# Handing PSUM banks from one stage to the next: which banks pass to whom, in a fused linear-attention and leaky-ReLU MLP kernel

## The chip, the cores and the metric

The kernel runs on one core of a Trainium2 chip. The metric is the device time of one launch in microseconds (us), the median of several runs. The engines are TensorE (PE, with its weight loads listed apart as PEld), VectorE (DVE), ScalarE (ACT), GpSimd (POOL) and SyncE (SP), which here only issues DMAs.

## The reference, cut to what matters

```python
def _attn_ref(q, k, v):                     # 8 batches, 8 heads, 576 tokens, 64 wide
    phi(x) = concatenate([relu(x) * cos_w, relu(x) * sin_w], axis=-1)
    kv = einsum('bhsf,bhsd->bhfd', phi(k), v)
    z = sum(phi(k), axis=2)
    num = einsum('bhsf,bhfd->bhsd', phi(q), kv)
    den = einsum('bhsf,bhf->bhs', phi(q), z)[..., None] + 1e-06
    return num / den

def _moe_ref(x, w_in, w_out):               # x: 4608 x 512, w_in: 512 x 2048, w_out: 2048 x 512
    h = x @ w_in
    g = maximum(0.01 * h, h)
    return g @ w_out
```

Inputs and output are float32; the kernel multiplies in float16 and accumulates in float32.

## The kernel before, in words

The 4608 rows are cut into nine groups of 512. Groups 0 to 7 are the first 512 tokens of each batch, and group 8 is made of the 64 last tokens of all eight batches (the "tail"). A group passes through these steps. `load_main`, `load_kvtail` and `load_qtail` bring q, k and v in as float32 (tiles `qst`, `kst`, `vst`, `ktl`, `vtl`, `qtl`). `k_part` and `q_part` make phi(k) and phi(q) in float16, `v_part` casts v; each of these can run on DVE or on ACT, and the strings of the table `ON` say which. `kv_all` multiplies phi(k) with v on PE and ACT copies the result. `q_transpose_dma` turns phi(q) by a transposing DMA, `num` multiplies it with kv on PE and divides on DVE (tiles `den`, `rden`, `xs`). `x_transpose_dma` turns the quotient; in group 2 alone PE turns it (`x_transpose`, line 490) and ACT copies it.

Then comes the MLP. Groups 0 and 1 are multiplied with w_in directly; from group 2 on w_in, and from group 1 on w_out, are multiplied by a seven-product (Strassen-Winograd) scheme on blocks of half the size. "Product one" in the words of the change is the multiplication with w_in, "product two" the one with w_out. In group 1 product one is `f1_pair` (line 833: pairs of 512-wide results in two PSUM banks, then a leaky ReLU by ACT at line 855). From group 2 on it is `p1(g, t, n, ...)`: set t of four, product n of seven, four matmuls 128 x 256 each, about which stand on ACT `seed` (line 892, copies a partial sum from one bank into another), `lrelu` (895), `u_copy` (902) and `u_lrelu` (909), and on DVE `u_add` (268). Product two is `p2(g, n, ...)` (line 975), with `o_copy` on ACT (994) and `o_add` on DVE (268). Sums of weight blocks (`w1_sums`, `w2_sums`), of x blocks (`x_sums`) and of g blocks (`g_sums`) run on DVE.

PSUM has eight banks of 512 float32 per partition, all in use. In the stage of groups 0 and 1 the pool `ps_h` has four (two tags of two banks, taken in turn by the pairs), `ps_o` has two single banks, and `ps_n` two. `x_transpose` of group 2 takes its bank from `ps_o`, `num` and `kv_all` theirs from `ps_n`. In the later stage four banks serve product one (`bank1`: two that the sets use in turn, then SEED and JOIN) and two serve product two (`bank2`). `open_banks` closes the first stage's pools and opens the later ones; a tile that lies on a bank of an old tile waits until that one's last reader is done. `open_seed` writes zeros into SEED by a matmul.

The order is a written table. Every call from group 1's product one on is put on a list with a place number out of `PLACE`, and the calls are issued in the order of these numbers. An engine works through its own instructions in that order, and SP its DMAs. The staging pool has three tiles for all loads of q, k and v from group 2 on: a load waits until a tile that has been read to the end is free, and what stands behind it on SP waits too.

Of the kernel before, what the change touches and what calls it, by code (L numbers as in the profile page):

```python
# [9 lines left out]
dt = mybir.dt  # L10
# [3 lines left out]
P = 128  # L14
# [4 lines left out]
def kernel(  # L19
# [26 lines left out]
    N2 = MAIN // 2  # L46
# [5 lines left out]
    first, first_ps = ExitStack(), ExitStack()  # L52

    def pool(name, bufs, space=None, stack=ctx):
# [5 lines left out]
    PS = bass.MemoryType.PSUM  # L60
# [15 lines left out]
    ps_of = {  # L76
        "h": pool("ps_h", 1, PS, first_ps),
        "o": pool("ps_o", 2, PS, first_ps),
        "n": pool("ps_n", 1, PS, first_ps),
    }  # L80
# [832 lines left out]
    SEED, JOIN = 2, 3  # L913
# [145 lines left out]
    bank1, bank2 = [], []  # L1059

    def open_banks():
        first_ps.close()
        ps_f1, ps_f2 = pool("ps_f1", 1, PS), pool("ps_f2", 1, PS)
        ps_of["n"] = pool("ps_m", 1, PS)
        for i in range(4):
            bank1.append(ps_f1.tile([P, 2, N2], dt.float32, name=f"ps_h{i}"))
        for i in range(2):
            bank2.append(ps_f2.tile([P, 2, N2], dt.float32, name=f"ps_o{i}"))

    def open_seed():  # L1070
        nc.tensor.matmul(
            bank1[SEED].rearrange("p h (a n) -> p (h a) n", n=P),
            lhsT=none,
            rhs=ident[:, None, :].broadcast_to([P, 4, P]),
        )
# [6 lines left out]
            16, 115, 251, 403, 570, 707, 852, 957,  # L1082
        ),
        "f1_pair": (
            52, 53, 46, 47, 43, 44, 39, 40, 25, 26, 57, 64, 17, 22, 35, 36,
        ),
        "open_banks": (
            72,
        ),
        "open_seed": (  # L1090
            73,
        ),
# [13 lines left out]
        ),  # L1106
        "seed": (
            81, 117, 149, 174, 237, 253, 304, 337, 399, 420, 452, 494, 535, 575, 609, 640, 690,
            710, 746, 790, 830, 865, 881, 911, 943, 967, 992, 1027,
        ),  # L1110
        "lrelu": (
# [4 lines left out]
        ),  # L1116
        "u_copy": (
# [4 lines left out]
        ),  # L1122
        "u_add": (
# [4 lines left out]
        ),  # L1128
        "u_lrelu": (
            154, 177, 247, 267, 288, 326, 377, 426, 444, 483, 556, 565, 602, 635, 696, 719, 768,  # L1130
            779, 828, 849, 888, 916, 931, 976, 998, 1025, 1048, 1065,
        ),
        "o_tiles": (
            97, 279, 406, 560, 720, 842, 974, 1066,
        ),
# [15 lines left out]
        ),  # L1151
        "o_copy": (
            98, 142, 171, 225, 280, 306, 348, 385, 407, 462, 475, 510, 561, 596, 617, 654, 721,
            756, 778, 820, 843, 886, 909, 951, 975, 1010, 1032, 1061, 1081, 1093, 1103, 1107, 1067,
            1086, 1096, 1114,
        ),
        "o_add": (
            160, 187, 230, 298, 349, 386, 417, 495, 521, 568, 634, 675, 730, 798, 825, 863, 919,
            953, 1003, 1036, 1056, 1087, 1111, 1119, 1090, 1098, 1116,
        ),  # L1160
        "o_store": (
            262, 342, 445, 423, 554, 646, 731, 682, 837, 900, 973, 989, 1080, 1057, 15, 111,
        ),
        "o_store_tail": (
            1092, 1112, 1115, 1120, 1117,
        ),
        "w1_sums": (
            102, 172, 67, 170, 175, 141,
        ),
        "w2_sums": (  # L1170
            10, 3, 42, 28, 38, 124, 164, 136,
        ),
        "g_sums": (
# [5 lines left out]
        ),  # L1179
        "kp_tiles": (  # L1180
            0, 69, 199, 358, 481, 622,
        ),
        "k_part": (
# [4 lines left out]
        ),  # L1188
        "v_part": (
            14, 13, 32, 129, 101, 103, 244, 255, 277, 323, 395, 389, 539, 553, 533, 672, 712, 663,  # L1190
        ),
        "kv_all": (
            41, 144, 281, 437, 566, 725,
        ),
        "q_part": (
# [4 lines left out]
        ),  # L1200
        "q_transpose_dma": (
            30, 21, 60, 9, 139, 92, 110, 89, 284, 260, 276, 295, 409, 413, 434, 422, 576, 538, 551,
            519, 698, 688, 748, 724, 805, 858, 872, 824,
        ),
# [138 lines left out]
```

## Time and profile before

| what | value |
|---|---|
| median of 3 runs | 271.7 us (271.56 to 272.0) |
| the profiled execution | 272.22 us, of which the span from its first to its last instruction is 270.4 us |
| granted TensorE clock | 1.000 |
| PE busy | 262.7 us |
| DVE busy | 207.7 us |
| ACT busy | 201.2 us |
| DMA, mean over the span | 211 GB/s, 57.05 MB |

Times below are counted from the span's start. Matmuls overlap in the trace, so PE looks busy while it waits a little. How long it stood is read from the starts: four matmuls of 128 x 256 start 0.437 us before the next thing (0.109 each), and four of 128 x 512 0.86 us before; what lies between two starts beyond that is waiting.

### The profile page before, as it was taken

The page shows a single profiled execution, that of the slowest core. Times are in us where ns is not written, and L with a number is a line of the kernel's source. Part 1 is how long each engine was busy: PE and PEld are TensorE (multiplying, and loading weights), DVE is VectorE, ACT ScalarE, POOL GpSimd, SP SyncE. Part 2 cuts the span into 40 slices and gives each one's busy share as a digit, 9 for nine tenths or more (in the row PEclk, how much of TensorE's full clock was granted, in tenths as well). Part 3 has the DMA queues.
Part 4 walks back from the last instruction along what each step waited for, and adds up shares of the span by engine and source line. Part 5 has one row for each costly group of instructions (what it writes and reads, how often), then busy time and mean ns, then how long its engine had stood idle before and what let it go on. Part 6 is the DMA issues. An engine that isn't in the chain of part 4 may idle for free.

```text
span 270.4 us, 6693 instructions
## 1 busy us (share of the span) xinstructions
PE 262.7 (97%) x2715; PEld 222.7 (82%) x2715; DVE 207.7 (77%) x429; ACT 201.2 (74%) x343; POOL 8.1 (3%) x20
## 2 busy tenths in 40 slices
PE   8899999998999999999999999999999999999994
PEld 3585565565889999999999999999988899999983
DVE  3984999996899988888877978888876845565651
ACT  7675545886899998987888977986777776774721
POOL 2131011000000000000000000000000000000000
PEclk9999999999999999999999999999999999999999
DMA  6999999989999999996999999789786060300134
GB/s 204 384 385 399 384 408 362 252 194 316 252 244 301 210 220 247 310 191 181 251 240 242 171 244 263 165 186 209 112 120 158 6 152 4 155 0 2 76 120 116
DMA packets 82654, 57.05 MB, mean 211 GB/s; under 512 B 54464, under 2 KB 75968, under 8 KB 82112
## 3 DMA queue, kind: packets, MB, share of 16 engines
q1 hardware_dynamic: 82320, 56.37, 83.2%
q8 instruction: 21, 0.34, 0.5%
q10 hardware_dynamic: 304, 0.26, 0.4%
q14 instruction: 9, 0.07, 0.1%
HBM read 36.70 MB, written 9.44 MB: 171 GB/s over the span
## 4 chain that ended last, share of the span: by engine, by line
PE 81%; DMA 10%; ACT 4%; SPq 1%; DVE 1%; issue 1%; POOL 0%; ACTq 0%; DVEq 0%
PE ps_o L975 30%; PE ps_h L882 29%; PE ps_o L543 5%; PE ps_h L506 4%; DMA vpr<-in_v_dram 3%; DMA vtl<-in_v_dram 3%; PE ps_h L975 3%; DMA qst<-in_q_dram 2%; PE ps_num L418 2%; PE ps_kv L317 2%; DMA qtl<-in_q_dram 2%; PE ps_hq L525 1%; PE ps_h L833 1%; ACT g L855 1%; PE ps_kvh L349 1%; PE ps_xth L475 1%
## 5 line engine op out<-in xcount | busy, mean ns | idle before, releaser
L975 PEld LDWEIGHTS <-g 128*128 128x128 f16 x640 | 62.3, 98 | 6.6
L268 DVE TENSOR_TENSOR u<-ps_h,u 128x512 f32<-128x512 f32 x56 | 38.5, 688 | 20.4 <-PE ps_h L882 15.3
L882 PEld LDWEIGHTS <-w 128*128 128x128 f16 x448 | 48.5, 114 | 1.2 <-issue 0.3
L975 PE MATMUL ps_o<-w,g 128*128 128x256 f16 x352 | 46.3, 273 | 0.0
L902 ACT COPY u<-ps_h 128x512 f32<-128x512 f32 x56 | 32.7, 586 | 14.9 <-PE ps_h L882 14.5
L882 PEld LDWEIGHTS <-wa 128*128 128x128 f16 x336 | 34.7, 106 | 2.6 <-issue 0.7
L895 ACT ACTIVATE g<-ps_h 128x512 f16<-128x512 f32 x56 | 33.0, 600 | 4.1 <-PE ps_h L882 4.0
L882 PE MATMUL ps_h<-xw,wa 128*128 128x256 f16 x224 | 33.4, 273 | 0.5 <-ACT ps_h L892 0.5
L882 PE MATMUL ps_h<-xw,w 128*128 128x256 f16 x224 | 33.3, 273 | 0.1
L882 PE MATMUL ps_h<-xT,w 128*128 128x256 f16 x224 | 33.1, 273 | 0.0
L975 PE MATMUL ps_o<-wb,g 128*128 128x256 f16 x232 | 32.0, 273 | 0.0
L909 ACT ACTIVATE g<-u 128x1024 f16<-128x1024 f32 x28 | 29.7, 1061 | 2.1 <-DVE u L268 1.9
L975 PEld LDWEIGHTS <-gs 128*128 128x128 f16 x256 | 24.5, 98 | 2.6
L994 ACT COPY ob<-ps_o 128x512 f32<-128x512 f32 (+1 forms) x32 | 18.0, 562 | 9.3 <-PE ps_o L975 9.1
L436 DVE TENSOR_TENSOR xs<-ps_num,rden 128x512 f16<-128x512 f32 x28 | 19.4, 692 | 1.6
L892 ACT COPY ps_h<-ps_h 128x512 f32<-128x512 f32 x28 | 16.2, 579 | 3.3 <-PE ps_h L882 2.9
L268 DVE TENSOR_TENSOR ob<-ps_o,ob 128x512 f32<-128x512 f32 (+1 forms) x22 | 14.8, 673 | 4.6 <-PE ps_o L975 3.5
L882 PE MATMUL ps_h<-xT,wa 128*128 128x256 f16 x112 | 16.8, 273 | 0.0
L975 PE MATMUL ps_o<-wb,gs 128*128 128x256 f16 x120 | 16.5, 273 | 0.0
L975 PE MATMUL ps_o<-w,gs 128*128 128x256 f16 x120 | 15.9, 272 | 0.0
L543 PE MATMUL ps_o<-w,g 128*128 128x512 f16 x64 | 15.6, 379 | 0.0
L833 PE MATMUL ps_h<-xT,w 128*128 128x512 f16 x64 | 14.8, 379 | 0.0
(116 smaller groups left out, 389.9 us busy)
## 6 DMA issues: line engine op xcount, KB each, us to landing
out_dram<-ob SPq DMA_DIRECT2D x16, 512.0 KB, 4.3
qst<-in_q_dram SPq DMA_DIRECT2D x7, 1024.0 KB, 6.7
kst<-in_k_dram SPq DMA_DIRECT2D x6, 1024.0 KB, 8.1
vst<-in_v_dram SPq DMA_DIRECT2D x6, 1024.0 KB, 7.6
w1st<-in_moe_w_in_dram SPq DMA_DIRECT2D x8, 512.0 KB, 11.2
w2st<-in_moe_w_out_dram SPq DMA_DIRECT2D x4, 1024.0 KB, 13.0
vpr<-in_v_dram SPq DMA_DIRECT2D x4, 576.0 KB, 10.9
kpr<-in_k_dram SPq DMA_DIRECT2D x3, 576.0 KB, 11.1
```

What stands on the lines that cost most here:

```text
L268: nc.vector.tensor_tensor(out=o, in0=a, in1=b, op=ALU.add)
L436: nc.vector.tensor_tensor(out=xs, in0=ps[:, :, 0 : 4 * NE].rearrange("p a (b e) -> p a b e", e=NE)[:, :, :, 0:D], in1=rden.rearrange("p (a ...
L506: nc.tensor.matmul(ps[:, n], lhsT=w1[m // 4][c // 2][:, c % 2, m % 4 + n : 512 : 4], rhs=st["xT", g][:, c], start=(c == 0), stop=(c == NKC ...
L543: nc.tensor.matmul(ps, lhsT=st["g", g][:, m, tt * P : (tt + 1) * P], rhs=w2[:, m, :], start=(m == 0), stop=(m == NFT - 1),)
L833: nc.tensor.matmul(ps, lhsT=w1[m // 4][c // 2][:, c % 2, m % 4 : 512 : 4], rhs=st["xT", g][:, c], start=(c == 0), stop=(c == NKC - 1),)
L882: nc.tensor.matmul(bank[:, p], lhsT=w(c), rhs=x_blocks(g)[n][:, c], start=(fresh and p == 0 and c == 0), stop=(c == 1), skip_group_check=True,
L892: nc.scalar.copy(bank1[bj], bank1[bi])
L895: nc.scalar.activation(st["g" + nm, g][:, 2 * t : 2 * t + 2], bank1[bi], AF.Lrelu)
L902: nc.scalar.copy(st["u", g, t][:, n], bank1[bi])
L909: nc.scalar.activation(st["gt", g][:, :, 1, 2 * t : 2 * t + 2], st["u", g, t], AF.Lrelu)
L975: nc.tensor.matmul(bank, lhsT=st[G2[n], g][:, m, pair * P : (pair + 1) * P], rhs=W2[n](m), start=(fresh and m == 0), stop=(m == NH - 1), s ...
L994: nc.scalar.copy(o_at(g, half_, col, pair), bank_of(bi, pair, pair is None))
```

## The change

Two things change. The first is which banks pass to whom. Before, all three first-stage pools are closed together. The four banks of `ps_h` become the four of product one, the two of `ps_o` (x's turns of group 2 among their users) the two of product two, and `ps_n` is opened anew. Now `ps_n` and `ps_o` stay open and only `ps_h` is closed. Two of its four banks become product two's `bank2`, two the banks that product one's sets use in turn, and SEED and JOIN are taken from `ps_o` when `open_seed` runs, one each. The second is the table: nearly all place numbers are new, and so are the letters of `ON`.

```diff
-    first, first_ps = ExitStack(), ExitStack()
+    first, pairs_ps = ExitStack(), ExitStack()
...
-        "h": pool("ps_h", 1, PS, first_ps),
-        "o": pool("ps_o", 2, PS, first_ps),
-        "n": pool("ps_n", 1, PS, first_ps),
+        "n": pool("ps_n", 1, PS),
+        "o": pool("ps_o", 2, PS),
+        "h": pool("ps_h", 1, PS, pairs_ps),
...
-    bank1, bank2 = [], []
+    bank1, bank2 = [None] * 4, []
 
     def open_banks():
-        first_ps.close()
-        ps_f1, ps_f2 = pool("ps_f1", 1, PS), pool("ps_f2", 1, PS)
-        ps_of["n"] = pool("ps_m", 1, PS)
-        for i in range(4):
-            bank1.append(ps_f1.tile([P, 2, N2], dt.float32, name=f"ps_h{i}"))
+        pairs_ps.close()
+        ps_f2, ps_f1 = pool("ps_f2", 1, PS), pool("ps_f1", 1, PS)
         for i in range(2):
             bank2.append(ps_f2.tile([P, 2, N2], dt.float32, name=f"ps_o{i}"))
+            bank1[i] = ps_f1.tile([P, 2, N2], dt.float32, name=f"ps_h{i}")
 
     def open_seed():
+        for i in (SEED, JOIN):
+            bank1[i] = psum("o", [P, 2, N2], dt.float32, f"ps_s{i}")
...
         "open_banks": (
-            72,
+            66,
         ),
         "open_seed": (
-            73,
+            85,
         ),
...
         "kv_all": (
-            41, 144, 281, 437, 566, 725,
+            41, 142, 278, 438, 579, 728,
         ),
...
         "loads": (
-            37, 68, 78, 93, 145, 207, 239, 316, 300, 412, 450, 478, 540, 593, 629,
+            31, 96, 81, 122, 174, 181, 229, 311, 369, 421, 406, 500, 593, 611, 626,
         ),
```

What the table moves is shown at three places. The first is SP's queue just after the last store of group 0's stage begins, up to the loads of batch 3 (`qst`, `kst`, `vst` are the main parts of q, k and v, `ktl` and `vtl` their tails, `qpT<-qp` the turns of phi(q)). Before:

```order
L386 DMA_TRANSPOSE qpT<-qp 128x8x128
L1001 DMA out_dram<-ob 128x1024
L386 DMA_TRANSPOSE qpT<-qp 128x8x128 x2
L104 DMA qst<-in_q_dram 128x8x256
L386 DMA_TRANSPOSE qpT<-qp 128x8x128
L104 DMA kst<-in_k_dram 128x8x256
L114 DMA ktl<-in_k_dram 64x4x64 x2
L104 DMA vst<-in_v_dram 128x8x256
L114 DMA vtl<-in_v_dram 64x4x64 x2
```

Of the change, at the same place:

```order
L386 DMA_TRANSPOSE qpT<-qp 128x8x128
L1001 DMA out_dram<-ob 128x1024
L386 DMA_TRANSPOSE qpT<-qp 128x8x128
L104 DMA qst<-in_q_dram 128x8x256
L386 DMA_TRANSPOSE qpT<-qp 128x8x128 x2
L104 DMA vst<-in_v_dram 128x8x256
L114 DMA vtl<-in_v_dram 64x4x64 x2
L386 DMA_TRANSPOSE qpT<-qp 128x8x128
L104 DMA kst<-in_k_dram 128x8x256
L114 DMA ktl<-in_k_dram 64x4x64 x2
```

The load of q goes ahead of one turn of phi(q), v goes ahead of k, and k goes behind the first turn of batch 3's own phi(q).

The second place is DVE at the divisions of group 2 (`den`, `rden` and `xs` are one division; `qp<-qst` is phi(q) of batch 3). Before:

```order
L436 TENSOR_TENSOR xs<-ps_num,rden 128x512
L257 TENSOR_SCALAR qp<-qst,cos_t 128x8x64
L257 TENSOR_SCALAR qp<-qst,sin_t 128x8x64
L433 TENSOR_SCALAR den<-ps_num 128x8
L435 RECIPROCAL rden<-den 128x8
L436 TENSOR_TENSOR xs<-ps_num,rden 128x512
L271 TENSOR_TENSOR gs_958<-g 128x1024
L433 TENSOR_SCALAR den<-ps_num 128x8
```

Of the change, from batch 3's first phi(q) on DVE:

```order
L257 TENSOR_SCALAR qp<-qst,sin_t 128x8x64
L271 TENSOR_TENSOR gs_953<-g 128x1024
L433 TENSOR_SCALAR den<-ps_num 128x8
L435 RECIPROCAL rden<-den 128x8
L436 TENSOR_TENSOR xs<-ps_num,rden 128x512
L257 TENSOR_SCALAR qp<-qst,sin_t 128x8x64
L257 TENSOR_SCALAR qp<-qst,cos_t 128x8x64
L433 TENSOR_SCALAR den<-ps_num 128x8
L435 RECIPROCAL rden<-den 128x8
L436 TENSOR_TENSOR xs<-ps_num,rden 128x512
```

Before, the first two phi(q) of batch 3 stand ahead of the third division; now one stands ahead of the second division and two ahead of the third.

The third place is ACT after the last leaky ReLU of group 1, where the first sums of group 2 pass from bank to bank (line 892 is `seed`, `vtail<-vtl` and `vmain<-vst` are casts of batch 3's v). Before:

```order
L892 COPY ps_h_1221<-ps_h_1219 128x512
L255 ACTIVATE qp<-qst,sin_t 128x8x64
L255 ACTIVATE kp<-kst,cos_t 128x8x64
L994 COPY ob<-ps_o_1223 128x2x256
L263 CAST vtail<-vtl 64x4x64 x2
L902 COPY u<-ps_h_1219 128x512
L895 ACTIVATE g<-ps_h_1221 128x512
L892 COPY ps_h_1221<-ps_h_1220 128x512
```

Of the change:

```order
L892 COPY ps_s_1250<-ps_h_1180 128x512
L263 CAST vmain<-vst 128x16x64
L994 COPY ob<-ps_o_1179 128x2x256
L902 COPY u<-ps_h_1180 128x512
L895 ACTIVATE g<-ps_s_1250 128x512
L892 COPY ps_s_1250<-ps_h_1182 128x512
L902 COPY u<-ps_h_1180 128x512
L255 ACTIVATE kp<-ktl,sin_t 128x4x64
```

The two casts of the v tail are gone from between the two seeds (both now stand on DVE), one cast of v's main part is there in their place, and phi(k) has moved behind.

More of the change, by code (lines that the diff above doesn't have):

```diff
@@ L1109 @@
-            710, 746, 790, 830, 865, 881, 911, 943, 967, 992, 1027,
+            89, 114, 145, 182, 225, 262, 289, 324, 371, 410, 436, 481, 530, 562, 602, 634, 682,
+            703, 754, 791, 813, 850, 881, 911, 943, 961, 994, 1011,
         ),
         "lrelu": (
[4 rows of a table removed]
[4 rows of a table added]
         ),
         "u_copy": (
[4 rows of a table removed]
[4 rows of a table added]
         ),
         "u_add": (
[4 rows of a table removed]
[4 rows of a table added]
         ),
         "u_lrelu": (
-            154, 177, 247, 267, 288, 326, 377, 426, 444, 483, 556, 565, 602, 635, 696, 719, 768,
-            779, 828, 849, 888, 916, 931, 976, 998, 1025, 1048, 1065,
+            159, 193, 245, 267, 299, 337, 392, 396, 453, 476, 529, 552, 605, 616, 694, 701, 752,
@@ L1132 @@
+            785, 820, 855, 906, 920, 948, 969, 995, 1016, 1049, 1058,
         ),
         "o_tiles": (
-            97, 279, 406, 560, 720, 842, 974, 1066,
+            99, 269, 429, 574, 709, 860, 980, 1064,
         ),
         "p2": (
[14 rows of a table removed]
[14 rows of a table added]
         ),
         "o_copy": (
-            98, 142, 171, 225, 280, 306, 348, 385, 407, 462, 475, 510, 561, 596, 617, 654, 721,
-            756, 778, 820, 843, 886, 909, 951, 975, 1010, 1032, 1061, 1081, 1093, 1103, 1107, 1067,
-            1086, 1096, 1114,
+            100, 137, 178, 220, 270, 317, 347, 388, 430, 458, 482, 527, 575, 613, 628, 674, 710,
@@ L1156 @@
+            748, 775, 809, 861, 889, 907, 940, 981, 1006, 1034, 1054, 1074, 1092, 1100, 1115, 1065,
+            1081, 1098, 1106,
         ),
         "o_add": (
-            160, 187, 230, 298, 349, 386, 417, 495, 521, 568, 634, 675, 730, 798, 825, 863, 919,
-            953, 1003, 1036, 1056, 1087, 1111, 1119, 1090, 1098, 1116,
+            101, 184, 233, 290, 363, 395, 446, 489, 536, 584, 635, 693, 727, 781, 825, 876, 914,
+            951, 1014, 1051, 1077, 1089, 1111, 1119, 1091, 1104, 1117,
@@ L1160 @@
         ),
         "o_store": (
-            262, 342, 445, 423, 554, 646, 731, 682, 837, 900, 973, 989, 1080, 1057, 15, 111,
+            342, 383, 477, 525, 566, 653, 766, 816, 848, 968, 1026, 1027, 1055, 1096, 188, 15,
         ),
         "o_store_tail": (
-            1092, 1112, 1115, 1120, 1117,
+            1095, 1112, 1116, 1120, 1118,
         ),
         "w1_sums": (
-            102, 172, 67, 170, 175, 141,
+            86, 65, 14, 18, 234, 157,
         ),
         "w2_sums": (
-            10, 3, 42, 28, 38, 124, 164, 136,
+            25, 42, 30, 43, 134, 45, 162, 136,
@@ L1172 @@
         ),
         "g_sums": (
[5 rows of a table removed]
[5 rows of a table added]
         ),
         "kp_tiles": (
-            0, 69, 199, 358, 481, 622,
+            7, 103, 189, 320, 448, 620,
         ),
         "k_part": (
[4 rows of a table removed]
[4 rows of a table added]
         ),
         "v_part": (
-            14, 13, 32, 129, 101, 103, 244, 255, 277, 323, 395, 389, 539, 553, 533, 672, 712, 663,
+            34, 32, 37, 98, 97, 82, 210, 208, 238, 414, 404, 412, 567, 515, 553, 665, 656, 677,
         ),
         "kv_all": (
-            41, 144, 281, 437, 566, 725,
+            41, 142, 278, 438, 579, 728,
@@ L1194 @@
         ),
         "q_part": (
[4 rows of a table removed]
[3 rows of a table added]
         ),
         "q_transpose_dma": (
-            30, 21, 60, 9, 139, 92, 110, 89, 284, 260, 276, 295, 409, 413, 434, 422, 576, 538, 551,
-            519, 698, 688, 748, 724, 805, 858, 872, 824,
+            60, 16, 46, 5, 164, 93, 116, 180, 302, 251, 319, 250, 389, 407, 460, 418, 580, 578,
+            554, 596, 755, 764, 743, 672, 838, 835, 852, 830,
         ),
         "num": (
-            54, 49, 61, 45, 178, 155, 189, 197, 320, 292, 301, 344, 474, 448, 488, 461, 612, 581,
@@ L1207 @@
-            632, 603, 765, 742, 781, 754, 841, 884, 873, 851,
+            61, 47, 69, 54, 175, 149, 165, 198, 303, 292, 344, 330, 466, 454, 501, 480, 600, 590,
+            633, 615, 757, 767, 746, 736, 898, 842, 887, 834,
         ),
         "x_transpose": (
-            62, 56, 66, 59,
+            71, 53, 77, 62,
         ),
         "x_sums": (
-            83, 94, 105, 120, 243, 246, 245, 250, 394, 396, 410, 397, 541, 543, 567, 555, 685, 694,
-            691, 695, 813, 814, 826, 835, 934, 935, 932, 936,
+            78, 79, 91, 87, 244, 254, 266, 258, 380, 381, 393, 401, 544, 547, 543, 571, 685, 690,
@@ L1215 @@
+            689, 706, 810, 811, 805, 836, 941, 942, 931, 950,
         ),
         "loads": (
-            37, 68, 78, 93, 145, 207, 239, 316, 300, 412, 450, 478, 540, 593, 629,
+            31, 96, 81, 122, 174, 181, 229, 311, 369, 421, 406, 500, 593, 611, 626,
         ),
         "x_transpose_dma": (
-            224, 201, 228, 233, 379, 305, 332, 388, 503, 471, 518, 486, 641, 620, 669, 643, 769,
-            770, 788, 762, 901, 929, 874, 921,
+            187, 186, 205, 209, 367, 332, 379, 372, 522, 484, 540, 533, 640, 629, 651, 645, 788,
@@ L1222 @@
+            789, 780, 772, 910, 870, 888, 844,
         ),
         "load_qtail": (
-            689, 706, 766, 733,
+            721, 678, 771, 670,
         ),
@@ L1228 @@
         "k_part": (
-            "VAVAVVVVVAAVAVVVVVAVVAVAVVAAVVAVAVAAVVVVAAVAVVVAVAVAVVAVVVVA"
+            "VVVVAVVAAVVAVAVVVVVAAAVVAAAVVVVVAAVAAVAVVVAAAVVVVAVVVVVAVAAV"
         ),
         "q_part": (
-            "AAAAVVAAVAAVVAAVAAVAVVAAAAVVAAVAVAAAVVVVAAVVAAVAVVAVAAVV"
+            "VVVAVAAAAAAVVVAAAAVAVVVAVVVAVVAVAVVVAAVAAAAAVVVVAAVAVAVA"
         ),
         "v_part": (
-            "VVAAVAAVAVAVVVAVVV"
+            "VAVAVVVAVVVVVAAVAV"
         ),
         "num": (
-            "VVVVVVAVVVVVAAAVVAAVVVVAAVAV"
+            "VAVVVAVVVVVAVAVAVAVVVAAVVVVV"
         ),
```

5 lines of the change are left out of this document (2 added, 3 removed), and 101 rows, old and new, of the table PLACE.

## The prediction

> **What bounds the kernel now.** First the page: which engine is full.
>
> ```profile
> PE 262.7 (97%) x2715; PEld 222.7 (82%) x2715; DVE 207.7 (77%) x429; ACT 201.2 (74%) x343; POOL 8.1 (3%) x20
> ```
>
> It is PE, with 2715 matmuls that the change leaves as they are. Its busy share hides short waits, so I went to the timeline of PE: start, duration (us), instruction, and in brackets idle time and its releaser.
>
> ```profile
> 50.39 7.07 PE L833 MATMUL ps_h<-xT,w 128*128 128x512 f16 x32
> 57.29 0.42 PE L317 MATMUL ps_kv<-vmain,kp 128*128 128x65 f16 x8
> ...
> 65.58 0.39 PE L490 MATMUL ps_xt<-ident,xs 128*128 128x128 f16 x4
> 66.87 0.41 PE L418 MATMUL ps_num<-kv,qpT 128*128 128x65 f16 x8 [0.90 <-DVE xs L436]
> 67.13 0.39 PE L490 MATMUL ps_xt<-ident,xs 128*128 128x128 f16 x4
> 67.35 1.03 PE L833 MATMUL ps_h<-xT,w 128*128 128x512 f16 x4
> 68.51 0.40 PE L490 MATMUL ps_xt<-ident,xs 128*128 128x128 f16 x4
> ...
> 75.53 0.60 PE L882 MATMUL ps_h<-xw,w 128*128 128x256 f16 x4
> 76.64 0.60 PE L882 MATMUL ps_h<-xw,wa 128*128 128x256 f16 x4 [0.50 <-ACT ps_h L892]
> 77.07 0.60 PE L975 MATMUL ps_o<-wb,gs 128*128 128x256 f16 x4
> ...
> 79.69 0.42 PE L317 MATMUL ps_kv<-vmain,kp 128*128 128x65 f16 x8
> ...
> 198.49 0.60 PE L882 MATMUL ps_h<-xw,wa 128*128 128x256 f16 x4
> 199.22 0.60 PE L882 MATMUL ps_h<-xw,w 128*128 128x256 f16 x4
> ```
>
> Four 128x512 cost 6.90/8 = 0.86 (50.39 to 57.29), four 128x256, a "block" below, 0.44 (76.64 to 77.07), four turns 0.22 (67.13 to 67.35). So PE stood 66.87 − 65.58 − 0.22 = 1.07 us before group 2's last `num`, 68.51 − 67.35 − 0.86 = 0.30 before its last turn of x, 76.64 − 75.53 − 0.44 = 0.67 in its first set, and 199.22 − 198.49 − 0.44 = 0.29 late. The starts from 50.39 to the end, gone through in the same way, show nothing else that lasts above 0.1. That is 2.3 us of waiting, 2.04 of it in the handover from group 1 to group 2.
>
> The Trainium skill (Perfetto Trace Analysis, Identifying the Most-Contended Engine) says that matmul busy time does not tell the headroom and that the share of LDWEIGHTS should be read for it. By that the 82% would leave some 48 us for a better order; the starts do not bear it out here, since the matmuls follow each other without a gap while the weight loads fill only part of the time.
>
> The chain of waits (start, length, what) says what is late in the handover:
>
> ```profile
> 58.01 6.70 DMA qst<-in_q_dram
> 64.71 0.03 ACTq L255
> ...
> 65.91 8.10 DMA vtl<-in_v_dram
> ...
> 74.04 0.41 ACT vtail L263
> ...
> 74.47 0.40 ACT vtail L263
> ...
> 74.90 0.58 ACT u L902
> 75.48 0.51 ACT g L895
> ...
> 76.01 0.58 ACT ps_h L892
> ```
>
> Two loads of batch 3 set it. Its q lands at 64.71, and phi(q), which stands on DVE ahead of a division, waits for it: the first two waits. Its v tail lands at 74.02; ACT stood for it, and the copy from bank to bank that PE needs at 76.64 was queued behind the two casts: the third.
>
> **The change part by part.** The bank swap adds and removes no instruction; it alters whose reader a bank waits for. Group 1's first `p2` now follows pair 0/1 of product one on its banks, so that pair's ReLU must be done; SEED and JOIN follow the last two turns of x.
>
> ```profile
> 65.41 1.00 ACT L855 ACTIVATE g<-ps_h 128x1024 f16<-128x1024 f32 x1
> 66.32 0.57 ACT L491 COPY xT<-ps_xt 128x512 f16<-128x512 f16 x1
> ```
>
> Between pair 0/1 and that `p2` the new order has a `num` (0.26, 66.87 to 67.13), a turn (0.22) and the last half of pair 12/13 (0.86), 1.34 us against a ReLU of 1.00: nothing, and if one copy (0.57) stands ahead on ACT, up to 0.3. SEED's turn has four blocks (1.75) as cover for its copy: nothing.
>
> The q load goes ahead of one turn of phi(q) on SP.
>
> ```profile
> 54.84 3.07 SPq L386 DMA_TRANSPOSE qpT<-qp  x2
> 58.01 0.90 SPq L104 DMA_DIRECT2D qst<-in_q_dram  x1
> ...
> 61.59 0.74 SPq L104 DMA_DIRECT2D kst<-in_k_dram  x1
> ...
> 65.22 0.60 SPq L104 DMA_DIRECT2D vst<-in_v_dram  x1
> ```
>
> ```profile
> 53.08 0.48 DVE L257 TENSOR_SCALAR kp<-kst,cos_t 128x512 f16<-128x512 f32 x1
> 53.48 0.48 DVE L257 TENSOR_SCALAR kp<-kst,sin_t 128x512 f16<-128x512 f32 x1
> 53.87 0.69 DVE L271 TENSOR_TENSOR wb<-w 128x1024 f16<-128x1024 f16 x1
> 54.47 0.48 DVE L257 TENSOR_SCALAR kp<-kst,cos_t 128x512 f16<-128x512 f32 x1
> ...
> 58.46 0.48 DVE L257 TENSOR_SCALAR qp<-qst,sin_t 128x512 f16<-128x512 f32 x1
> ```
>
> In a row on DVE a phi costs 0.40 (53.08 to 53.48) and a sum or cast of 1024 0.60 (53.87 to 54.47). Before, the load waited for the last phi(q) of batch 2, which ends at 58.94. In the new order that one is eighth on DVE, five phis and two short sums ahead of it, so done at about 54.6; SP then decides, with one turn (3.07/2) behind 54.84: 56.4, or 1.6 to 2.5 us earlier. At the same latency (6.70) q lands near 63.1. DVE's list up to there sums to 9.05 us from 51.5 (10 phis, 5 large sums, a cast, tails and short sums), then it must wait for the first `num` anyway, whose division ends near 62.9. So phi(q) is late by 0.2, the next division is not held up, and the waits of 1.07 and 0.30 go; between zero and 0.8 us may come back, the far end if q lands 1 us later.
>
> The v tail's casts leave ACT, where both seeds stood around them. On DVE they fall after x's sums, and v is issued right behind the turns, at about 60 in place of 65.22. ACT's cast of v's main part between the seeds finds its data landed.
>
> ```profile
> 78.18 1.05 ACT L263 CAST vmain<-vst 128x1024 f16<-128x1024 f32 x1
> ```
>
> It costs 1.05 there; the second seed is needed only ten blocks after the first set opens (4 us), so it is hidden. The 0.67 goes.
>
> What is late next: k. It moves from 61.59 to behind the first turn of batch 3's own phi(q), which waits for phi(q) on ACT (a ReLU, a copy and two phis after 62): about 65.5. Queued behind it on SP are the next turns and batch 4's loads, needed later than 80.
>
> ```profile
> DMA to landing us min/median/max: 7.2/7.6/7.9
> ```
>
> At 7.9 (the two k loads nearest to this stretch took 7.2 to 7.9) k lands at 73.4, its tails a little later. DVE reaches phi(k) near 74.9: the last division ends near 68.9, then come four g sums, x's four sums, the casts of v, a weight sum and an `o_add`, some 6 us at the rates above. Six phis and a tail (2.7) end at 77.6. PE reaches `kv_all(3)`, at 79.69 before, with 24 blocks ahead of it instead of 23: 79.69 − 2.04 + 0.44 = 78.1. The cover is 0.5; if k or DVE is 1 us late, PE waits 0.5 there. For the handover as a whole I leave 0.4 of new waiting (bounds 0 and 1.3: the 0.8 and the 0.5), nearer to the low end because each step comes out with a little cover.
>
> From 80 on everything moves, but no work is added: by the letters of `ON` DVE gains some 1.4 us and ACT loses 2.2, against 60 us that each is idle. Counting the blocks that lie between the last write of a bank and its next use, the closest cases are as close as before (two blocks for a copy, three for a copy and an add), so I see no new wait that must be. Before, 190 us of this cost 0.29. I keep that and add 0.3 for a new order (bounds: −0.29, and 1.5, five times the row).
>
> The tail is the same: two blocks of `p2`, an add, a store.
>
> ```profile
> 264.94 1.91 PE L975 MATMUL ps_h<-w,g 128*128 128x256 f16 x16
> ...
> 266.89 0.42 DVE L268 TENSOR_TENSOR ob<-ps_h,ob 128x256 f32<-128x256 f32 x1 [0.45 <-PE ps_h L975]
> ```
>
> Sum, against the profiled execution of 272.22 (span 270.40): −2.04 + 0.4 + 0.3 = −1.3, so 270.9. The median of the runs shown, 271.7, is 0.5 below that execution: **270.4**.
>
> **The rivals.** (a) The wait moves to k: k lands at 75 or later, phi(k) starts late, PE waits 1 to 1.5 us before `kv_all(3)` and the gain is 0.3 or less: 271.4. For it: k is issued 4 us later than before, behind a wait. Against: v, not k, was last before, and its tail landed at 74.02, which PE's place of 78.1 can just bear. The Trainium skill (DMA: Bandwidth & Descriptors, Queues, rings and completion order) says that each DMA engine takes descriptors in ring order, so k would queue behind v's bytes; no row here separates the two.
>
> (b) Slower: batch 5's k. The new order puts its first phi(k) on DVE ten places after the load (43 before), and three `u_add` queue behind it.
>
> ```profile
> kst<-in_k_dram SPq DMA_DIRECT2D x6, 1024.0 KB, 8.1
> w2st<-in_moe_w_out_dram SPq DMA_DIRECT2D x4, 1024.0 KB, 13.0
> ```
>
> The tile is free near 103.5; at 8.1 us k lands at 111.6, when DVE, two us behind its list there, just gets to it. The `u_add` of the third set must be done by about 115. From 10.5 us of latency on each us is a us on PE; at 13.0, what loads of this size took at the start, 2.5, so 270.4 + 2.5 = 272.9. Loads of q for batches 6 and 7 stand as close. Against: the DMA engines are as loaded as before, not as at the start.
>
> (c) The swap does not do what it says: the first `p2` waits for the pair's ReLU that it now follows. ACT two instructions late gives 1 us, and the divisions behind it on PE move too: 271.5. Against: 1.34 us of cover.
>
> **How the numbers follow.** Forecast 0.56 (270.4, own range 269.4, where all 2.3 are gone, to 271.2); (a) 0.15, (c) 0.07, (b) 0.17; other losses in the long stage 0.05, taken as slower. What a measurement can tell is about 0.2%, 0.54 us, so faster means below 271.16. Faster: 0.54 of the forecast and 0.06 of (a) and (c): 0.60. Within: 0.02 + 0.14 = 0.16. Slower: 0.24, with 0.02 of (a) and (c). Range 269.3 to 273.0: up to (b)'s time.
>
> **What would show it.** Right: no PE gap over 0.3 between 60 and 80, the q load issued before 57.5, `kv_all(3)` starting at 78 to 78.6, no cast of `vtl` on ACT between the first two copies of L892. Wrong: a gap before `kv_all(3)` (a); DVE idle for `kst` between 108 and 116 and a PE wait for L268 after it (b); PE waiting for ACT L855 at the first L975 after group 1 (c). The forecast fails if waits after 80 sum to more than 1.5 us.

## The result, and the profile after

| what | before | after |
|---|---|---|
| median, measured side by side (11 runs each) | 271.48 us (270.42 to 272.01) | 270.17 us (269.62 to 271.03) |
| after / before, with its 95% interval | | 0.9955 [0.9934, 0.9976] |
| the profiled execution (its span) | 272.22 us (270.4) | 270.13 us (268.3) |
| PE busy | 262.7 us | 262.5 us |
| PE waiting after 50 us, from the starts | 2.33 us | 0.12 us |

The kernel became 1.31 us faster by the medians and 2.09 us by the two profiled executions. The section on the prediction says why these differ.

First the page of the kernel after, its engines:

```profile
PE 262.5 (98%) x2715; PEld 222.9 (83%) x2715; DVE 209.2 (78%) x436; ACT 198.6 (74%) x336; POOL 7.7 (3%) x20
```

The matmuls are the same 2715 and as busy. DVE has 1.5 us more work and ACT 2.6 less, as the new letters say; both stay below 80% of the span. Next the view of waits for PE (line and tile, what it waited for; total, times, longest):

```profile
PE ps_idle L190 <- DVE blank L183: 1.2, 1, 1.2
PE ps_kvh L349 <- POOL vpair L265: 0.4, 1, 0.4
PE ps_xth L475 <- DVE xp L436: 0.4, 1, 0.4
```

All three lie before 17 us, in code that the change leaves alone. `ps_num <- xs` (0.9 before) and `ps_h L882 <- ps_h L892` (0.5 before) are gone. The same place on PE's timeline as in the prediction, after the change:

```profile
63.44 0.42 PE L418 MATMUL ps_num<-kv,qpT 128*128 128x65 f16 x8
63.70 1.89 PE L833 MATMUL ps_h<-xT,w 128*128 128x512 f16 x8
65.42 0.42 PE L418 MATMUL ps_num<-kv,qpT 128*128 128x65 f16 x8
65.68 0.39 PE L490 MATMUL ps_xt<-ident,xs 128*128 128x128 f16 x4
65.90 1.03 PE L833 MATMUL ps_h<-xT,w 128*128 128x512 f16 x4
66.77 0.60 PE L975 MATMUL ps_o<-w,g 128*128 128x256 f16 x4
67.20 0.42 PE L418 MATMUL ps_num<-kv,qpT 128*128 128x65 f16 x8
67.46 0.60 PE L975 MATMUL ps_o<-w,g 128*128 128x256 f16 x4
67.89 0.39 PE L490 MATMUL ps_xt<-ident,xs 128*128 128x128 f16 x4
68.12 1.04 PE L975 MATMUL ps_o<-w,g 128*128 128x256 f16 x8
68.99 0.39 PE L490 MATMUL ps_xt<-ident,xs 128*128 128x128 f16 x4
...
77.29 0.60 PE L975 MATMUL ps_o<-wb,g 128*128 128x256 f16 x4
77.85 0.60 PE L882 MATMUL ps_h<-xT,w 128*128 128x256 f16 x4
78.29 0.42 PE L317 MATMUL ps_kv<-vmain,kp 128*128 128x65 f16 x8
```

Every start follows the one before it by the price of the work between (0.26 a `num`, 0.22 a turn, 0.44 a block, 0.86 a half pair). The largest gap is 77.85 − 77.29 − 0.44 = 0.12. Note where the four blocks of `p2` (L975) stand: one between the third and the last `num`, one behind that `num`, two behind the next turn of x.

The loads of batch 3, on SP's queue, and the phi(k) that waits for the last of them:

```profile
55.30 0.79 SPq L104 DMA_DIRECT2D qst<-in_q_dram  x1
...
62.03 0.52 SPq L104 DMA_DIRECT2D vst<-in_v_dram  x1
...
67.21 0.59 SPq L104 DMA_DIRECT2D kst<-in_k_dram  x1
...
74.98 0.87 DVE L257 TENSOR_SCALAR kp<-kst,cos_t 128x512 f16<-128x512 f32 x2
75.58 0.51 ACT L255 ACTIVATE kp<-ktl,sin_t 128x256 f16<-128x256 f32 x1 [0.27 <-DMA ktl<-in_k_dram]
...
77.22 0.48 DVE L257 TENSOR_SCALAR kp<-kst,sin_t 128x512 f16<-128x512 f32 x1
```

q goes out 2.7 us earlier than before (58.01), k 5.6 us later (61.59). DVE finds k landed when it gets there, and the last phi(k) is done near 77.7, 0.6 us before `kv_all(3)` at 78.29.

### The profile page after: what moved, and what is told of

It reads as the page before. It is cut to its first block, busy times and chain, and to the rows that moved or that the text cites. A ratio compares the mean times of both kernels' runs of the same rounds, so it can differ in the third digit from the quotient of the medians.

```text
span 268.3 us, 6694 instructions
## 1 busy us (share of the span) xinstructions
PE 262.5 (98%) x2715; PEld 222.9 (83%) x2715; DVE 209.2 (78%) x436; ACT 198.6 (74%) x336; POOL 7.7 (3%) x20
## 4 chain that ended last, share of the span: by engine, by line
PE 82%; DMA 13%; SPq 3%; DVE 1%; POOL 0%; issue 0%
PE ps_o L975 34%; PE ps_h L882 18%; PE ps_s L882 14%; DMA w2st<-in_moe_w_out_dram 6%; PE ps_h L833 5%; DMA w1st<-in_moe_w_in_dram 4%; PE ps_num L418 3%; DMA kpr<-in_k_dram 3%; PE ps_kv L317 2%; SPq L131 2%; PE ps_h L975 2%; PE ps_o L543 1%; PE ps_s L975 1%; PE ps_kv L324 1%; DVE w L265 0%; SPq L163 0%
## 5 line engine op out<-in xcount | busy, mean ns | idle before, releaser
L975 PEld LDWEIGHTS <-g 128*128 128x128 f16 x640 | 62.1, 98 | 6.8
L268 DVE TENSOR_TENSOR u<-ps_s,u 128x512 f32<-128x512 f32 x56 | 38.5, 687 | 19.3 <-PE ps_s L882 18.4
L882 PEld LDWEIGHTS <-w 128*128 128x128 f16 x448 | 48.7, 114 | 1.0
L975 PE MATMUL ps_o<-w,g 128*128 128x256 f16 x352 | 46.8, 273 | 0.0
L882 PEld LDWEIGHTS <-wa 128*128 128x128 f16 x336 | 34.4, 106 | 1.9
L882 PE MATMUL ps_h<-xw,w 128*128 128x256 f16 x224 | 32.5, 273 | 0.0
L975 PE MATMUL ps_o<-wb,g 128*128 128x256 f16 x232 | 31.5, 273 | 0.0
L975 PEld LDWEIGHTS <-gs 128*128 128x128 f16 x256 | 24.6, 98 | 2.6
L892 ACT COPY ps_s<-ps_h 128x512 f32<-128x512 f32 x28 | 16.2, 579 | 6.2 <-PE ps_h L882 5.7
L895 ACT ACTIVATE g<-ps_s 128x512 f16<-128x512 f32 x28 | 16.8, 601 | 5.1 <-PE ps_s L882 4.8
L895 ACT ACTIVATE g<-ps_h 128x512 f16<-128x512 f32 x28 | 16.7, 600 | 5.3 <-PE ps_h L882 5.1
L882 PE MATMUL ps_s<-xT,wa 128*128 128x256 f16 x112 | 16.8, 273 | 0.0
L882 PE MATMUL ps_h<-xw,wa 128*128 128x256 f16 x112 | 16.8, 273 | 0.0
L882 PE MATMUL ps_s<-xw,wa 128*128 128x256 f16 x112 | 16.8, 273 | 0.0
L882 PE MATMUL ps_s<-xT,w 128*128 128x256 f16 x112 | 16.8, 273 | 0.0
L882 PE MATMUL ps_h<-xT,w 128*128 128x256 f16 x112 | 16.7, 273 | 0.0
L975 PE MATMUL ps_o<-wb,gs 128*128 128x256 f16 x120 | 16.5, 273 | 0.0
```

Of the source, the lines that this page charges most:

```text
L268: nc.vector.tensor_tensor(out=o, in0=a, in1=b, op=ALU.add)
L882: nc.tensor.matmul(bank[:, p], lhsT=w(c), rhs=x_blocks(g)[n][:, c], start=(fresh and p == 0 and c == 0), stop=(c == 1), skip_group_check=True,
L892: nc.scalar.copy(bank1[bj], bank1[bi])
L895: nc.scalar.activation(st["g" + nm, g][:, 2 * t : 2 * t + 2], bank1[bi], AF.Lrelu)
L975: nc.tensor.matmul(bank, lhsT=st[G2[n], g][:, m, pair * P : (pair + 1) * P], rhs=W2[n](m), start=(fresh and m == 0), stop=(m == NH - 1), s ...
```

## The experiments

Times are compared with runs of the kernel before on the same chip, made together with them. "Gaps" are PE's waits after 50 us, from the starts, as in the prediction. In the edits a number is the place in the list, and the call stands behind it.

**The kernel before, once more.** No edit.

> The kernel before, unchanged, for a second profile of it. Theory A (the 2.04 us of PE waiting in the handover are what the change took away): PE waits again 1.5 to 2.3 us between 60 and 80, at the last num, the last turn of x and the first set of group 2, and the time is within 0.2% of the kernel before. Rival B (the waits hang on how fast the DMAs happen to land, and the profiled execution was a slow one): a sum under 1.3 us.

Measured: 271.25 us, ratio 0.9999 [0.9983, 1.0015], span 269.0. PE's timeline of this second profile:

```profile
64.54 0.42 PE L418 MATMUL ps_num<-kv,qpT 128*128 128x65 f16 x8
...
66.27 0.41 PE L418 MATMUL ps_num<-kv,qpT 128*128 128x65 f16 x8
...
66.75 1.03 PE L833 MATMUL ps_h<-xT,w 128*128 128x512 f16 x4
67.91 0.40 PE L490 MATMUL ps_xt<-ident,xs 128*128 128x128 f16 x4
```

The 1.07 before the last `num` is 0.17 here (66.27 − 64.54 − 0.26 − 0.22 − 0.86 − 0.22), the 0.30 before the last turn is there again (67.91 − 66.75 − 0.86), and the waits of 0.67 and 0.29 are missing. So 0.47 of the 2.04 us comes back in another execution, and the other 1.6 does not have to.

**Batch 3's q load earlier, on the kernel before.**

```diff
-29   q_part(2, 2, 0)
-33   q_part(2, 2, 1)
-37   loads(3, 'q')
+20.2 q_part(2, 2, 0)
+20.4 q_part(2, 2, 1)
+29.5 loads(3, 'q')
```

> Before, with batch 2's two last phi(q) moved ahead on DVE and the load of batch 3's q moved ahead of two turns of phi(q) on SP; banks as before. Theory A (the q load sets the first two waits): the waits of 1.07 and 0.30 fall to 0.3 or less together; the loads behind it on SP move up 1 to 1.5 us too, so the third wait (0.67) shrinks below 0.3; time 1.0 to 1.8 us below before. Rival B (the spacing of the num blocks by a single PSUM tile, or the banks themselves, set them): 0.8 us or more of the 1.37 stays, time within 0.5 us of before.

Measured: 272.04 us, ratio 1.0024 [1.0002, 1.0046], span 270.5. By SP's queue the load went ahead of one turn of phi(q), as in the change, and not of two; it was issued at 56.04. Gaps: 0.28 before `kv_all(2)`, whose phi(k) on DVE now stand behind the two phi(q) that the edit moved, 0.17 and 0.31 at the two old places, 0.17 (at 72.64), 0.64 and 0.66 in group 2's first set, and 0.45 at 199.33. What ACT and PE did at the 0.64 and the 0.66:

```profile
73.99 0.83 ACT L263 CAST vtail<-vtl 64x256 f16<-64x256 f32 x2 [0.92 <-DMA vtl<-in_v_dram]
74.85 0.59 ACT L902 COPY u<-ps_h 128x512 f32<-128x512 f32 x1
75.49 0.60 PE L882 MATMUL ps_h<-xw,w 128*128 128x256 f16 x4 [0.47 <-ACT u L902]
75.97 0.57 ACT L892 COPY ps_h<-ps_h 128x512 f32<-128x512 f32 x1
76.59 0.60 PE L882 MATMUL ps_h<-xw,wa 128*128 128x256 f16 x4 [0.50 <-ACT ps_h L892]
```

Two readings follow. DVE's first phi(q) ran at 63.81 without waiting, and the gaps of 0.17 and 0.31 stayed: q's landing does not make these two. And the prediction's third wait is real: a v tail that lands late holds ACT 0.92 us, and both copies behind it make PE wait.

**The casts of the v tail later, on the kernel before; then both edits.**

```diff
-103   v_part(3, 2)
+117.5 v_part(3, 2)
```

> Before, with ACT's two casts of batch 3's v tail moved behind the second copy from bank to bank; banks and loads as before. Theory A (the casts, which wait for the v tail, hold up that copy): the third wait (0.67) goes, the first two (1.37) stay, time 0.4 to 0.7 us below before. Rival B (the copy is held up by something else, or kv_all(3) now waits for the casts): as much waiting as before, moved, time within 0.3 us.

> The two edits together (q load early, v tail casts late), banks as before. Theory A (the handover's waits are those of two loads, and the banks matter nothing): all handover waits together below 0.4 us, time 1.3 to 2.0 us below before, level with the change. Rival B (part of the gain needs the other banks): 0.6 us or more of waiting stays and the change is faster than this by that much.

Measured: later casts alone 271.44 us, ratio 1.0003 [0.9984, 1.0021], gaps 0.17, 0.30 and 0.41 (at 77.15, where PE waits for a `u_copy` that now stands behind the casts), and 0.11 at 198.29. Both edits 271.54 us, ratio 1.0021 [1.0001, 1.0041], the same three gaps (0.41 at 77.39). With the casts moved the 0.64 and 0.66 of the run above are gone and 0.41 is there in their place; the move is not all of that difference, since the v tail also landed earlier, at 73.65 in place of 74.18. On the old order neither edit nor both bring a gain.

**The two halves of the change apart.** First the new banks with the table of before; then the new table with the banks of before, where the opening and four blocks of `p2` have to move behind the last turn of x, since they take the turns' banks there.

```diff
-66 open_banks()
-67 p2(1, 2, 0, 0)
-70 p2(1, 1, 0, 0)
-75 p2(1, 1, 1, 0)
-76 p2(1, 1, 0, 1)
 77 x_transpose(2, 2)
+77.1 open_banks()
+77.2 p2(1, 2, 0, 0)
+77.3 p2(1, 1, 0, 0)
+77.4 p2(1, 1, 1, 0)
+77.5 p2(1, 1, 0, 1)
```

> The change's banks with the table of before (places and letters). In that order pair 12/13 of product one ends last, and it is its banks that product two of group 1 now takes. Theory A (banks alone bring nothing): the three handover waits stay, and a wait of 0.4 to 0.8 us for ACT L855 comes in at the first L975 after group 1; time 0.3 to 0.9 us above before. Rival B (banks matter): waits fall by 0.5 us or more, time below before.

> The change's table with the banks of before. Since those can only be handed over after the last turn of x, the opening and the first four blocks of product two move behind it; all else as in the change. Theory A (the new banks are what lets four blocks, 1.75 us, stand between the last divisions, and so cover them): PE waits 1.0 to 1.8 us for DVE xs before the last num and the last turn of x; time 0.8 to 1.8 us above the change. Rival B (the loads alone did it): waits of 0.3 us or less there, time level with the change.

Measured, as a table of two by two (ratio to before):

| | table of before | table of the change |
|---|---|---|
| banks of before | 1 | 1.0075 [1.0049, 1.0101] |
| banks of the change | 0.9997 [0.9979, 1.0014] | 0.9955 [0.9934, 0.9976] |

Each ratio is against runs of the kernel before that were made with it. The banks alone give nothing, the table alone loses, and only together they win. PE with the new banks and the old table:

```profile
67.97 0.38 PE L1071 MATMUL ps_s<-ident,none 128*128 128x512 f16 x1
68.72 1.47 PE L975 MATMUL ps_o<-w,g 128*128 128x256 f16 x12 [0.36 <-ACT g L855]
```

The first `p2` directly behind the last pair waits for that pair's ReLU, 68.72 − 67.97 − 0.22 = 0.53 us: rival (c), in an order that gives it no cover. The 0.17 and 0.30 of before are there too, and 0.21 and 0.23 at 143 and 198 us, in the long stage. PE with the new table and the old banks:

```profile
67.04 1.03 PE L833 MATMUL ps_h<-xT,w 128*128 128x512 f16 x4
68.29 0.41 PE L418 MATMUL ps_num<-kv,qpT 128*128 128x65 f16 x8 [0.23 <-DVE xs L436]
68.55 0.38 PE L490 MATMUL ps_xt<-ident,xs 128*128 128x128 f16 x4
69.94 0.40 PE L490 MATMUL ps_xt<-ident,xs 128*128 128x128 f16 x4 [1.00 <-DVE xs L436]
70.93 2.83 PE L975 MATMUL ps_o<-w,g 128*128 128x256 f16 x24 [0.60 <-ACT xT L491]
```

Without the four blocks in between PE waits 0.39 for the division before the last `num`, 1.17 for the next one, and 0.77 for the copy of the turn at 68.55, on whose bank the first `p2` now stands (ACT began that copy at 70.29, behind two phi(q)): 2.33 us. This profile also has 1.1 us more before 51 us than that of the change, in code that is the same. By the view of waits PE stood 0.8 longer for the cast of an early load of v and 0.8 at 20.4 for the cast of a weight block, and made up a part of it by 51 us; the last run below, with another table, has the second of these waits too. So of the 0.75% that the table alone loses, about half may belong to the start of the kernel; what the order shows by itself is the 2.33 us against 0.12 with the new banks.

**The loads' timing in the changed kernel.** In the first run two turns of phi(q) are moved ahead of the q load, so that it stands behind them again; in the second the casts of the v tail are back on ACT.

```diff
+30.1 q_transpose_dma(2, 2)
+30.2 q_transpose_dma(2, 0)
 31   loads(3, 'q')
-46   q_transpose_dma(2, 2)
-60   q_transpose_dma(2, 0)
```

```diff
-82 v_part(3, 2, 'V')
+82 v_part(3, 2, 'A')
```

> The change with the load of batch 3's q moved behind two turns of phi(q) on SP, where before had it. Theory A: q lands about 2.5 to 3 us later, DVE stands at phi(q) ahead of the divisions of group 2, PE waits 0.8 to 2.0 us for xs before nums or turns of x, and k, issued later too, may add a wait before kv_all(3); time 0.8 to 2.5 us above the change. Rival B (the new order has cover enough): waits below 0.4 us, time level.

> The change with the two casts of batch 3's v tail on ACT, ahead of the first copy from bank to bank, instead of on DVE. Theory A (what counted was that the v tail landed late, and v is now issued 5 us earlier): no wait, time within 0.2% of the change. Rival B (ACT has no room for the casts there): PE waits 0.3 to 0.8 us for ACT L892 in the first set, time 0.3 to 0.8 us above.

Measured: q late 271.78 us, ratio 1.0018 [0.9996, 1.004]; casts on ACT 270.49 us, ratio 0.9956 [0.9938, 0.9973]. The first one's q load was issued at 58.53 in place of 55.30, and the timeline of SP, DVE and PE shows its price:

```profile
58.53 0.57 SPq L104 DMA_DIRECT2D qst<-in_q_dram  x1
...
64.02 1.89 PE L833 MATMUL ps_h<-xT,w 128*128 128x512 f16 x8
...
64.77 0.49 DVE L257 TENSOR_SCALAR qp<-qst,sin_t 128x512 f16<-128x512 f32 x1 [1.46 <-DMA qst<-in_q_dram]
...
67.05 0.41 PE L418 MATMUL ps_num<-kv,qpT 128*128 128x65 f16 x8 [1.14 <-DVE xs L436]
```

PE waits 1.31 us (67.05 − 64.02 − 1.72) and all of the gain is gone. So the prediction's mechanism of the first wait is right where it strikes: late q, late phi(q), late division, `num` waits. The casts on ACT cost one gap of 0.25 (at 73.27) and nothing that the ratio shows (0.9956 beside 0.9955), not 0.67 us: v is issued at 62.1 there, against 65.22 in the first profile of before, and ACT did not wait for it.

**The change once more, and batch 5's k later.** No edit in the first; in the second:

```diff
-311 loads(5, 'k')
 319 q_transpose_dma(4, 2)
+320 loads(5, 'k')
```

> The change once more, for a second profile. The question is which of its savings hold from one execution to the next, since the kernel before showed 2.04 us of PE waiting in the handover in its first profile and only 0.5 in its second. Theory (the new order covers the divisions whatever the loads do): no PE gap above 0.15 us between 60 and 80 here either, kv_all(3) starting at 78 to 79 once the head's waits are taken off, median 270.2 to 270.6. Rival (the first profile of the change was a lucky one): gaps of 0.3 to 1 us before num, before a turn of x or before kv_all(3), span above 269.0.

> The change, with the load of batch 5's k behind one turn of phi(q) of batch 4 more (issue at about 104 to 106.5 in place of 101.3). Rival (b) of the prediction gave this place a cover of some 2 us, after which each us of lateness is a us of PE. In the profile of the change DVE reaches the first phi(k) at 111.1 without waiting, 9.8 us after the issue. If (b) prices it rightly: k lands near 112 to 114, DVE waits 1 to 2.5 us for kst near 111, the sums of the third set behind it are late and PE waits 0.5 to 2.5 us between 112 and 120; median 270.7 to 272.5. If there is more slack on PE than (b) said: DVE waits but PE does not, and the time stays at 270.2 to 270.5.

Measured: the change again 270.1 us, ratio 0.9951 [0.9926, 0.9976], span 268.4, one gap of 0.16 (before the block ahead of `kv_all(3)`). On this chip the kernel before lay between 270.41 and 273.85 us (29 runs), the change between 269.64 and 271.32 (12 runs). k later: 270.42 us, ratio 0.9947 [0.9921, 0.9973].

```profile
105.34 0.53 SPq L104 DMA_DIRECT2D kst<-in_k_dram  x1
...
108.61 0.58 SPq L1001 DMA_DIRECT2D out_dram<-ob  x1
...
111.31 0.88 DVE L257 TENSOR_SCALAR kp<-kst,sin_t 128x512 f16<-128x512 f32 x2 [0.16 <-DMA kst<-in_k_dram]
...
116.11 0.59 ACT L994 COPY ob<-ps_o 128x512 f32<-128x512 f32 x1 [0.58 <-DMA out_dram<-ob]
...
116.75 1.03 PE L975 MATMUL ps_o<-wb,g 128*128 128x256 f16 x8
```

In the change this load was issued at 101.27 and landed 6.5 us later, at 107.79, so 3.3 us before DVE came to it. Issued 4.07 us later it landed 5.9 us after its issue, and DVE waited 0.16 us. PE had one gap above 0.15, of 0.31 at 116.75, but not for k: ACT's copy ahead of that block waited 0.58 for a store, which SP, now with the k load shortly ahead of it, issued at 108.61 in place of 107.85. So rival (b) was wrong in the landing time (111.6 forecast); the 2 us of cover that it put behind the landing were not reached, and what a us beyond them costs is not shown for this load.

**Is it one chain of `num` and division?** On the kernel before, with its banks and loads, PE gets more work between the `num`. The first run has only one half pair between the second and the third; the second run has two.

```diff
-45   num(2, 3)
-49   num(2, 1)
-52   f1_pair(1, 0)
-54   num(2, 0)
-57   f1_pair(1, 12)
-60   q_transpose_dma(2, 2)
-61   num(2, 2)
+43.5 num(2, 3)
+46.5 num(2, 1)
+49.3 f1_pair(1, 0)
+49.5 num(2, 0)
+55   q_transpose_dma(2, 2)
+56.5 f1_pair(1, 12)
+57.5 num(2, 2)
```

The second run differs from the first in two places:

```diff
-49.3 f1_pair(1, 0)
-56.5 f1_pair(1, 12)
+48   f1_pair(1, 12)
+50.5 f1_pair(1, 0)
```

> The kernel before with its own banks, where the four num of group 2 stand further ahead among the pairs of group 1 and two full 128x512 halves lie between num and num; loads unchanged. Theory (what PE stands for in a typical run is the one chain num, division, next num, 1.73 us from num to num, with too little PE work in between: 1.56 and 1.34 of it before): the gaps of 0.17 and 0.30 before the last num and the last turn of x shrink to 0.1 or less together, the span is about 0.4 below that of the kernel before, 0.1 to 0.2% faster at most. The old banks then would cost nothing by themselves, and what the change gains beyond that comes from elsewhere. Rival (the loads of batch 3 set these waits): both gaps stay, 0.17 and 0.30. Third possibility: num of pair 2 now waits for its turned phi(q), issued near 59 on SP, and a new gap of 0.3 to 1.5 us stands before it.

> The same test as num_early with the places mended: there only one half (0.86 us of PE) stood between the second and the third num, and PE waited 0.62 us for the division, num to num 1.73 us. Here two halves stand between each num and the next (2.0 us from num to num), one half and two turns between the last num and the last turn of x; banks and loads are those of the kernel before. Theory (the one chain num, division, next num sets these waits): no gap above 0.1 before any num, at most 0.15 before the last turn of x; so 0.3 to 0.4 us of PE waiting less than the kernel before had in its second profile, and no more from the old banks than that. Rival (the loads, or the old banks, set them): gaps of 0.17 and 0.30 or more stay. Either way the time is within 0.3% of the kernel before, since the other waits of that order, those that come and go with the landing of the loads, are left in it.

Measured: the first 272.14 us, ratio 1.0015 [0.9987, 1.0042]. Its second and third `num`:

```profile
61.39 0.42 PE L418 MATMUL ps_num<-kv,qpT 128*128 128x65 f16 x8
61.64 1.03 PE L833 MATMUL ps_h<-xT,w 128*128 128x512 f16 x4
...
62.28 0.69 DVE L436 TENSOR_TENSOR xs<-ps_num,rden 128x512 f16<-128x512 f32 x1
...
63.12 0.41 PE L418 MATMUL ps_num<-kv,qpT 128*128 128x65 f16 x8 [0.45 <-DVE xs L436]
```

With 1.11 us of PE work between them, PE waits 0.62 (63.12 − 61.39 − 1.11), and the distance is 1.73 us, the same 1.73 as from 64.54 to 66.27 in the second profile of before. This profile has other gaps too: 0.19 before the third turn, 0.21 before the last one, 0.22 at 199.1, and 0.91 at 144.13, where ACT had stood 1.72 us for batch 6's k ahead of a copy that PE needs. So a load that lands late in the long stage costs PE as well, on the old table.

The second run came out slower: 273.07 us, ratio 1.0052 [1.0032, 1.0072]. No `num` waits in it, as the theory said, but two other large gaps opened (0.15 at 64.41 and 0.34 at 200.22 besides). The first of them:

```profile
67.88 0.38 PE L490 MATMUL ps_xt<-ident,xs 128*128 128x128 f16 x4 [0.89 <-ACT xT L491]
```

This turn is the third on two banks, and the first one's copy stood on ACT behind a ReLU: 1.05 us. The second: the zeros for SEED waited 1.00 us for the last pair's ReLU (0.8 of it `ps_h L1071 <- ACT g L855` in its view of waits), since pair 12/13, begun earlier, now lay on SEED's bank; the last turn kept 0.21. So with the old banks PE can be given work between the `num`, but in this order the turns and the opening then waited for ACT instead. No run shows whether another order on the old banks does without waits.

## Why the prediction was right, and where it was not

**The bound and the place** hold. From the first L833 to the start of the last row of `p2` (16 matmuls of L975 in the tail) it takes 212.2 to 212.4 us plus the gaps: 214.55 with 2.33 (before), 212.87 with 0.47 (before once more), 213.53 with 1.31 (q late), 212.32 with 0.12 (the change). PE's waits account for what this stage gains or loses.

**The removed waits (−2.04).** As the difference of the two profiled executions this is right. As the gain of the change it is too large, because the first execution was a poor one of a kernel that varies. Of the 2.04, the five later profiles on the old table in which no `num` and no turn of x was moved each have 0.47 at the two old places; the rest comes when q (0.90 in the first profile) or the v tail (0.67 there, 1.3 with q earlier) lands late, and goes when not. The median of before, 271.48, lies between its two profiled executions (272.22 and 270.84).

**The step that named the cause** was half wrong. The prediction gave the waits of 1.07 and 0.30 to the q load alone. An earlier q left 0.17 and 0.31 standing. What sets these is the chain through one PSUM tile: `num`, `den`, `rden`, `xs`, and only then the next `num`, 1.73 us (1.64 to a turn of `xs`, 66.27 to 67.91), while the old order gave PE 1.56 us of work between the third and the last `num`, and 1.34 before the last turn. The new order gives 1.78 and 1.79 there (65.42 to 67.20, and 67.20 to 68.99), because blocks of `p2` may stand between. They may, because the new banks let group 1's product two open before the last turn of x. The prediction costed the bank swap at nothing and looked only for what it might cost. The two by two table shows that neither half gains without the other.

How the 1.31 us of the medians divide is only in part shown. The chain is worth 0.31 to 0.35 (0.47 less the 0.12 and 0.16 that the change keeps). The rest must then be late landings that the new order meets less often, since it issues q at 55.3 and v at 62.0, against 57.2 to 58.0 and 63.8 to 65.2 in the two profiles of before; this is argued from single profiles. Taking away either support loses the whole gain, q's early issue (1.0018) as well as the banks (1.0075), so the two shares do not simply add.

**The q load**: predicted issue 56.4, measured 55.30; the waits went, and they come back in the new order when q is late (1.31 us). One reading behind it does not hold: that before the load waited for the last phi(q) of batch 2. The second profile of before has the load ahead of that phi(q), and so has the first (58.01 and 58.46):

```profile
57.22 0.52 SPq L104 DMA_DIRECT2D qst<-in_q_dram  x1
...
58.31 0.48 DVE L257 TENSOR_SCALAR qp<-qst,sin_t 128x512 f16<-128x512 f32 x1
```

What stood ahead of it on SP was the turns alone. The run with the earlier q load moved two phi(q) as well, which the load did not need, and its gap of 0.28 comes from them.

**The v tail**: the mechanism was seen again in a run of its own, but the term of 0.67 is one that appears when v is late. With v issued at 62.03 (predicted 60) and the casts left on ACT it is 0.25.

**The swap's cover** was predicted as 1.34 us against a ReLU of 1.00. ACT's timeline of the kernel after has this ReLU of pair 0/1:

```profile
65.62 1.02 ACT L855 ACTIVATE g<-ps_h 128x1024 f16<-128x1024 f32 x1 [0.34 <-PE ps_h L833]
```

It ends 0.13 before the first `p2` at 66.77: no wait, with less to spare than the 0.34 forecast. Rival (c) fell here; with the new banks in the old order, which gives no cover, it cost 0.53.

**New waiting in the handover (+0.4)** measured 0.12, in the second profile 0.16. k went out at 67.21, 1.7 us later than forecast, and DVE still came to it at 74.98 (forecast 74.9) and was done near 77.7 (77.6); the cover of 0.5 was 0.6. Rival (a) fell.

**The long stage (+0.3)** measured −0.29: the 0.29 at 199 is gone, and no new gap came. That this one went is a single execution against another: it is missing in the second profile of before as well. Rival (b) fell: k landed at 107.79, not 111.6, DVE reached it at 111.09 without a wait, and with the load 4 us later DVE waited 0.16.

**The sum.** Against the profile it was −1.3 and measured −2.09: the two allowances were 0.28 and 0.59 too high, and 0.1 was lost before 50 us. Against the median, 0.5 was taken off since the profiled execution of before lay that far above it; but the profiled execution of the change lies at its median (270.13 and 270.17). The two errors cancel down to 0.2 us between 270.4 and 270.17. That the size came out so near is in part luck.

**The share of weight loads.** It went from 82% to 83%, while the waits after 50 us went from 2.33 to 0.12. The Trainium skill (Perfetto Trace Analysis, Identifying the Most-Contended Engine) names this share, together with the share of the peak rate that the matmuls reach, for judging TensorE's headroom. The traces do not bear out the share as a measure of what a better order can win: the 17% that it leaves after the change would be some 45 us, an estimate, where the starts leave 0.12 us of waiting after 50 us.

## What to carry to other kernels

A wait of PE in one profile should be seen in a second one before its length is put into a sum: part of it can be a transfer's luck and part is set by a chain, and only the second part is there in every execution. For a chain through one PSUM tile, add up its steps and count the matmul work that the order puts between two turns of it; where work is lacking, ask which banks the next stage would need in order to lend some. A swap of banks that adds and removes nothing can still be what makes an order possible, so test banks and order apart and together.

## What was not expected of the hardware

The same kernel, unchanged, stood 2.33 us in one profiled execution and 0.47 in the next, and 29 runs of it spread over 3.4 us (270.41 to 273.85); the changed one over 1.7 us (269.64 to 271.32, 12 runs). With 11 runs of each side by side the spreads were 1.6 and 1.4 us, so it is not shown that the change narrows them. Loads of the same 1 MB from one queue did not take the same time either: in the profile of the change the six main loads of k took 6.0 to 9.4 us from issue to landing, batch 5's among them 6.5, and 5.9 when it was issued 4.07 us later.
